# Transposed squares in 3 KB runs, and one interleaved sequence up to chunk 2

## The chip, the cores and the metric

The kernel runs on one core of one Trainium2 chip. The metric is device microseconds of that core for one launch. The inputs lie in the chip's memory and the output goes back there.

## The reference

```python
# attention: x (4, 4096, 192), weight_gen (4, 4096, 8 heads, 7 taps), all float32
w = softmax(weight_gen, axis=-1)
x_pad = six rows of zeros ahead of each batch of x
out[b, s, h, :] = sum over k of w[b, s, h, k] * x_pad[b, s + k, h, :]    # 24 columns a head
# feed-forward on the 16384 rows: w_in (192, 2048), w_out (2048, 192)
h = out @ w_in
g = maximum(0.01 * h, h)
result = g @ w_out
```

It is a causal convolution of seven taps whose weights differ by row and head, and then two matrix products with a leaky ReLU between them. Both products are made at more than the precision of one pass: every operand is cut into an upper half (the type fp32r) and the rest, and the products of the halves are summed.

## The kernel before

**Chunks, pairs, steps.** The 16384 rows are 32 chunks of 512. Chunk c has the convolution (`conv_ops`), the split into halves (`split_h`, `split_l`), the transposition (`squares` and `spread_squares`, which leave it in the tile `xx`), and eight *pairs* i of 256 of the 2048 hidden columns. Step n = 8c + i is `step(n)`: `mm1` makes the hidden columns of pair i into two PSUM tiles `hp` (18 matmuls), `act` turns each into `gh` (ACT) and `gl` (DVE), and `mm2` multiplies an earlier pair's `gh` and `gl` into `po` (20 matmuls). In a step with i = 0 two pairs go through `mm2` together (40 matmuls) and finish the chunk before, which `evacuate` then copies to `ot` in pieces of four copies on ACT per step. TensorE (PE) does nothing else but these matmuls.

**Transposition.** For every chunk but the first, DVE transposes 32 x 32 squares inside 32 partitions (two instructions, one for each half, `split` to `sq`), and then 16 DMAs carry the squares from `sq` to the partitions of `xx` where they belong. `xx` has two buffers, `sq` and `split` one. The first chunk goes through TensorE instead (`first_transposes`).

**Preparing the weights.** In the first 75 us the engines also turn the two weight matrices, which come as float64 words, into halves: 16 pieces (eight of w_in, called IN below, eight of w_out, called OUT), each in five stages: r (two reads on ACT), w (three DVE instructions at L119, L121 and L125), o (rounding up, at L133), u (upper half, L152 or L154) and l (lower half, L158). A stage has a DVE form (O, U, L) beside the usual one on GpSimd (POOL) or ACT. `mm1` of pair i waits for IN i, `mm2` for OUT i.

**What sets the order.** Instructions are queued on each engine in the order in which the Python code calls them. The string START is that order up to some step: each letter is one action (a stage of the next weight piece, one convolution operation of chunk 0 (d, e, g) or 1 (p), the first transposition T, the split c and v, the transposes t and m and the DMAs x of chunk 1), and `s` is the next step. START holds ten steps, 0 to 9; from there `step` itself calls everything, with these lines for a chunk c + 1:

```python
m = i - {1: 5, 2: 4, 3: 2}.get(c, 1)
if i == 0: feed(c + 1, 2 * K)              # the rest of the convolution of chunk c + 1, on POOL
if m == 0: split_h(c + 1); split_l(c + 1, nc.gpsimd)
if m == 1: squares(c + 1, 0); squares(c + 1, 1); spread_squares(...)
if m >= 0: feed(c + 2, 3)
```

So chunk 2 is split in step 13 (i = 5 of chunk 1) and transposed and sent in step 14, chunk 3 in steps 20 and 21. The softmax weights come in eight pieces of two chunks; piece 1 (chunks 2 and 3) is worked on in steps 0, 1, 6 and 7.

**Waits that the order makes.** `ps_h` has four PSUM banks, given in turn to every tile that asks: the two `hp` of a step and the tile `t` of every w. A tile waits until the one four before it is done with, so w's that stand between two steps decide which `gl` or which w the next step waits for. DMAs of the SP queue are issued one after the other.

Of the kernel before, what the change touches and what calls it, by code (L numbers as in the profile page):

```python
# [9 lines left out]
F32 = mybir.dt.float32  # L10
# [7 lines left out]
P = 128  # L18
# [6 lines left out]

C0 = 1

START = "ASdeegdegddegddeeeeddegpggrgwgdgeOgdrepggeeduprgldpdwopTwurwpsLorwrpopurOulupplwsLwOprsOurlwpwuorsouurlwlOrwlurwlswprooucLouwtUvmosrLwrUlswoUOlxUlsLss"


@with_exitstack
def conv_attention_moe_kernel(
# [140 lines left out]
    def load_weights(q):  # L173
        r0 = piece[q] * R
        wt[q] = win.tile([P, R, HK], F32, tag="wt", name="wt")
        nc.sync.dma_start(out=wt[q], in_=w_rows[:, r0:r0 + R, :])
# [26 lines left out]
    def softmax_max(q):  # L203
        mx[q] = win.tile([P, R * H, 1], F32, tag="mx", name="mx")
        sm[q] = win.tile([P, R * H, 1], F32, tag="sm", name="sm")
        nc.vector.tensor_reduce(out=mx[q], in_=grouped(q, ALL), axis=AX.X, op=ALU.max)  # L206

    def softmax_sub(q, eng):
        eng.tensor_tensor(  # L209
            out=grouped(q, ALL), in0=grouped(q, ALL), in1=spread(mx[q], ALL), op=ALU.subtract  # L210
        )
# [53 lines left out]
    xx = {}  # L265

    def new_xx(c):
        xx[c] = xtp.tile([P, 2, NB, TOK], F32R, tag="xx", name="xx", bufs=2)

    def first_transposes():  # L270
        new_xx(0)
        for b in range(NB):
            t = ps_h.tile([P, TOK], F32, tag="h", name="ta")
            for j in range(J):
                nc.tensor.transpose(  # L275
                    out=t[:, j * P:(j + 1) * P],
                    in_=twice[:, j, b].rearrange("p u d -> p (u d)"), identity=ident,
                )
            h, l = xx[0][:, 0, b, :], xx[0][:, 1, b, :]
            nc.scalar.copy(out=h, in_=t)  # L280
            nc.vector.tensor_tensor(out=l, in0=t, in1=h.bitcast(F32), op=ALU.subtract)

# [2 lines left out]
    def split_h(c):  # L285
        split[c] = xtp.tile([P, 2, J, D], F32R, tag="split", name="split")
        nc.scalar.copy(out=split[c][:, 0], in_=att[c])  # L287

    def split_l(c, eng):
        h, l = split[c][:, 0], split[c][:, 1]  # L290
        eng.tensor_tensor(out=l, in0=att.pop(c), in1=h.bitcast(F32), op=ALU.subtract)  # L291

    def squares(c, i):

        if i == 0:
            sq[c] = xtp.tile([P, 2, D // BK, J, BK], F32, tag="sq", name="sq")
        nc.vector.transpose(  # L297
            out=sq[c][:, i],
            in_=split[c][:, i].bitcast(F32).rearrange("p j (b d) -> p b j d", d=BK),
        )  # L300

    def spread_squares(c, engs):

        new_xx(c)
        dst = xx[c].bitcast(F32).rearrange("p i b t -> p (i b) t")
        n = 0
        for k in range(NK):
            src = sq[c][k * BK:(k + 1) * BK].rearrange("p i (b v) j t -> p v (i b) (j t)", v=2)
            for g in range(NK):
                engs[n % len(engs)].dma_start(  # L310
                    out=dst[g * BK:(g + 1) * BK, :, k * P:(k + 1) * P], in_=src[:, g % 2]
                )
                n += 1

# [2 lines left out]
    def mm1(q):  # L317

        c, i = divmod(q, NQ)
        h, l = xx[c][:, 0], xx[c][:, 1]  # L320
        passes = []
        for b in range(NB):
            passes += [(wi_h[:, b, i, :], h[:, b, :]), (wi_h[:, b, i, :], l[:, b, :])]
            passes.append((wi_l[:, b, i, :], h[:, b, :]))
        for u in range(2):
            hp[2 * q + u] = ps_h.tile([P, TOK], F32, tag="h", name="hp")
        for m, (w, r) in enumerate(passes):
            for u, s in enumerate(HALVES):
                nc.tensor.matmul(  # L329
                    out=hp[2 * q + u], lhsT=w[s], rhs=r[s],  # L330
                    start=(m == 0), stop=(m == len(passes) - 1),
                )
# [90 lines left out]
    with tc.manual_schedule():  # L423
        warm = const.tile([P, 1], F32, name="warm")
        nc.vector.memset(warm, 0.0)
        nc.scalar.activation(out=warm, in_=warm, func=AF.Exp)
        load_weights(0)
        load_words(order[0], nc.scalar)
        load_rows(0)
        for key in order[1:4]:  # L430
            load_words(key)
        make_identity(nc, ident)
        sm_q = {}
        for q in range(1, NPIECE):
            sm_q[max(0, 2 * q - 3)] = q
        NP = NCH * NQ

        convs = []

        def feed(c, n):  # L440

            while n > 0:
                if not convs or convs[-1][1] is None:
                    last = convs[-1][0] if convs else 1
                    if last + 1 > min(c, NCH - 1):
                        return
                    convs.append([last + 1, conv_ops(last + 1, nc.gpsimd, "tmp")])
                ops = convs[-1][1]
                if next(ops, ops) is ops:
                    convs[-1][1] = None  # L450
                else:
                    n -= 1

        outs = {}

        def step(q):

            c, i = divmod(q, NQ)
            if i == 0 and c in sm_q:
                load_weights(sm_q[c])  # L460
                load_rows(sm_q[c])
            if i == 1 and c in sm_q:
                softmax_max(sm_q[c])
                softmax_sub(sm_q[c], nc.gpsimd)
            mm1(q)
            for u in range(2):
                act(2 * q + u)
            if i == 0 and q > 0:
                mm2([2 * q - 4, 2 * q - 3])
                mm2([2 * q - 2, 2 * q - 1])  # L470
                outs[c - 1] = evacuate(c - 1)
                run(outs[c - 1], 1)
            elif i >= 2:
                mm2([2 * q - 4, 2 * q - 3])
            if i > 0 and c - 1 in outs:
                run(outs[c - 1], 4)
            if c > 0:

                m = i - {1: 5, 2: 4, 3: 2}.get(c, 1)
                if i == 0:  # L480
                    feed(c + 1, 2 * K)
                if c + 1 < NCH:
                    if m == 0:
                        split_h(c + 1)
                        split_l(c + 1, nc.gpsimd)
                    if m == 1:
                        squares(c + 1, 0)
                        squares(c + 1, 1)
                        spread_squares(c + 1, [nc.sync, nc.scalar] if c == 1 else [nc.sync])
                if m >= 0:  # L490
                    feed(c + 2, 3)
            if i == 6 and c in sm_q:
                softmax_exp(sm_q[c])
            if i == 7 and c in sm_q:
                softmax_sum(sm_q[c])
                softmax_div(sm_q[c], nc.gpsimd)

        w0 = ps_o.tile([P, J * H, K], F32, tag="m0", name="w0")
        conv0 = dict(
            d=conv_ops(0, nc.vector, "h", 0, 2, ps_h, w0),  # L500
            e=conv_ops(0, nc.vector, "h", 2, J - C0, ps_h, w0),
            g=conv_ops(0, nc.gpsimd, "tmp0", J - C0, J),
            p=conv_ops(1, nc.gpsimd, "tmp"),
        )
        n = 0
        for what in START:
            if what in stages:
                prepare(what)
            elif what == "A":
                softmax_max(0)  # L510
                softmax_sub(0, nc.vector)
                softmax_exp(0)
            elif what == "S":
                softmax_sum(0)
                softmax_div(0, nc.vector, slice(0, J - C0), w0[:, 0:(J - C0) * H, :])
                softmax_div(0, nc.gpsimd, slice(J - C0, R))
            elif what in conv0:
                run(conv0[what], 1)
            elif what == "T":
                first_transposes()  # L520
            elif what == "c":
                split_h(1)
            elif what == "v":
                split_l(1, nc.gpsimd)
            elif what in "tm":
                squares(1, "tm".index(what))
            elif what == "x":
                spread_squares(1, [nc.sync])
            elif what == "s":
                step(n)  # L530
                n += 1
        for n in range(n, NP):
            step(n)
        mm2([2 * NP - 4, 2 * NP - 3])
        mm2([2 * NP - 2, 2 * NP - 1])
        run(evacuate(NCH - 1))
# [33 lines left out]
```

## Time and profile before

| what | us |
|---|---|
| median of three runs | 1217.04 (1215.18 to 1217.26) |
| the profiled execution's own time | 1211.91 |
| its span, first to last instruction | 1210.1 |
| PE busy | 1154.7 (95%) |
| ACT, POOL, DVE busy | 883.1, 802.3, 607.1 |
| PE waits for the DMAs `xx<-sq` | 15.9 in 5 waits |

The busy share of PE is an average over stages. The profile is best read by stretches: the start, until the first step of chunk 1; then the stretches up to the first steps of chunks 2, 3 and so on; and the tail behind the last matmul.

### The profile page before, as it was taken

Reading aid. Unit: us, or ns where it says so; the run is one execution under the profiler, and the core shown is the slowest. Engines: PE = TensorE matmul, PEld = TensorE weight load, DVE = VectorE, ACT = ScalarE, POOL = GpSimd, SP = SyncE. Lnnn points to the kernel's source line nnn. Section 1 sums busy time; section 2 is a strip of 40 time slices with the busy share of each in tenths; the row PEclk is TensorE's granted clock in tenths of the full one; section 3 lists DMA queues with packets and bytes.
Section 4 is the critical chain, followed back from the end, with each engine's and each line's share of the span. In section 5 each row is a group of like instructions: output and inputs, shape, how many; then the busy total and the mean of one; then the engine's idle time right before and its main releaser. Section 6 shows DMA issues by size and latency. Waiting matters only on the chain.

```text
span 1210.1 us, 24837 instructions
## 1 busy us (share of the span) xinstructions
PE 1154.7 (95%) x9740; PEld 958.6 (79%) x9740; DVE 607.1 (50%) x905; ACT 883.1 (73%) x1936; POOL 802.3 (66%) x524
## 2 busy tenths in 40 slices
PE   2887989999999999999999999999999999999997
PEld 1676868888888888888888888888888888888885
DVE  8973435445454444545444454444445444544443
ACT  3855647887777778777777777778877777877775
POOL 7868378766666876666687666678766668866300
PEclk9899989999999999999999999999999999999999
DMA  4543042422324242232423323242331324222210
GB/s 146 156 119 66 1 119 66 118 58 52 98 48 120 66 108 65 54 93 54 119 66 92 81 49 93 58 120 66 77 93 44 96 64 119 66 66 43 48 43 27
DMA packets 118307, 94.94 MB, mean 78 GB/s; under 512 B 9391, under 2 KB 111791, under 8 KB 116398
## 3 DMA queue, kind: packets, MB, share of 16 engines
q1 hardware_dynamic: 116110, 92.18, 30.1%
q10 hardware_dynamic: 2080, 1.18, 0.5%
q8 instruction: 76, 1.25, 0.4%
q14 instruction: 41, 0.34, 0.1%
HBM read 31.98 MB, written 12.58 MB: 37 GB/s over the span
## 4 chain that ended last, share of the span: by engine, by line
PE 91%; DVE 3%; SPq 2%; DMA 1%; ACT 1%; issue 1%; POOL 0%; ACTq 0%; DVEq 0%
PE po L357 47%; PE hp L329 43%; SPq L310 2%; DMA xx<-sq 1%; ACT hp L336 1%; DVE sq L297 0%; DVE h L246 0%; DVE gl L340 0%; ACT gh L338 0%; DVE acc L256 0%; DVE t L121 0%; DVE bits L125 0%; DVE t L119 0%; PE ta L275 0%; DMA wt<-in_weight_gen_dram 0%
## 5 line engine op out<-in xcount | busy, mean ns | idle before, releaser
L357 PE MATMUL po<-gh,wo 64*128 64x512 f32 x3072 | 633.4, 393 | 0.0
L340 DVE TENSOR_TENSOR gl<-hp,gh 128x512 fp32r<-128x512 f32 x512 | 353.0, 690 | 542.0 <-ACT gh L338 540.8
L329 PE MATMUL hp<-xx,wi_h 64*128 64x512 f32 x3072 | 581.5, 396 | 25.7 <-DMA xx<-sq 15.9
L357 PE MATMUL po<-gl,wo 64*128 64x512 f32 x2048 | 554.4, 392 | 0.0
L357 PEld LDWEIGHTS po<-gh,wo 64*128 64x128 f32 x3072 | 479.3, 185 | 59.7
L329 PEld LDWEIGHTS hp<-xx,wi_h 64*128 64x128 f32 x3072 | 435.0, 186 | 91.4 <-issue 15.4
L329 PE MATMUL hp<-xx,wi_l 64*128 64x512 f32 x1536 | 476.2, 396 | 0.0
L336 ACT ACTIVATE hp<-hp 128x512 f32<-128x512 f32 x512 | 300.2, 586 | 203.2 <-PE hp L329 203.2
L357 PEld LDWEIGHTS po<-gl,wo 64*128 64x128 f32 x2048 | 377.9, 185 | 39.7
L256 POOL TENSOR_TENSOR acc<-acc,tmp 128x768 f32<-128x768 f32 (+1 forms) x191 | 347.2, 1818 | 14.3
L338 ACT CAST gh<-hp 128x512 fp32r<-128x512 f32 x512 | 300.5, 587 | 16.2
L329 PEld LDWEIGHTS hp<-xx,wi_l 64*128 64x128 f32 x1536 | 285.3, 186 | 30.5 <-DVE wi_l L158 0.4
L246 POOL TENSOR_TENSOR tmp<-xt,wt 128x768 f32<-128x768 f32 (+1 forms) x192 | 290.7, 1514 | 12.2
L395 ACT COPY ot<-z 32x128 f32<-32x128 f32 x752 | 223.4, 297 | 11.6 <-DVE z L379 0.9
L291 POOL TENSOR_TENSOR split<-acc,split 128x768 fp32r<-128x768 f32 x31 | 57.4, 1850 | 185.3 <-ACT split L287 185.3
L370 ACT COPY sa<-po 128x512 f32<-128x512 f32 x64 | 37.6, 587 | 59.9 <-PE po L357 59.9
L209 POOL TENSOR_TENSOR wt<-wt,mx 128x448 f32<-128x448 f32 x15 | 14.7, 977 | 99.2 <-DVE mx L206 96.6
L371 DVE TENSOR_TENSOR sa<-po,sa 128x512 f32<-128x512 f32 x64 | 43.0, 672 | 46.3 <-ACT sa L370 46.3
L297 DVE STREAM_TRANSPOSE sq<-split 128x768 f32<-128x768 f32 x62 | 56.8, 953 | 0.0
L246 POOL TENSOR_TENSOR acc<-xt,wt 128x768 f32<-128x768 f32 (+1 forms) x32 | 48.5, 1515 | 0.2
L395 POOL COPY ot<-z 32x128 f32<-32x128 f32 x8 | 2.7, 332 | 62.0 <-DVE z L379 61.8
L222 POOL TENSOR_TENSOR wt<-wt,sm 128x448 f32<-128x448 f32 (+1 forms) x16 | 15.3, 959 | 19.4 <-DVE sm L219 19.4
(50 smaller groups left out, 266.1 us busy)
## 6 DMA issues: line engine op xcount, KB each, us to landing
xx<-sq SPq DMA_DIRECT2D x488, 96.0 KB, 2.3
xt<-in_x_dram SPq DMA_DIRECT2D x14, 1344.0 KB, 6.5
out_dram<-ot SPq DMA_DIRECT2D x32, 384.0 KB, 2.5
wt<-in_weight_gen_dram SPq DMA_DIRECT2D x16, 224.0 KB, 3.2
wo_raw<-in_moe_w_out_dram SPq DMA_DIRECT2D x8, 384.0 KB, 3.5
wi_raw<-in_moe_w_in_dram SPq DMA_DIRECT2D x14, 192.0 KB, 3.4
xt<-in_x_dram SPq DMA_DIRECT2D x1, 960.0 KB, 5.0
xx<-sq ACTq DMA_DIRECT2D x8, 96.0 KB, 3.8
```

Source lines behind the costliest of these rows:

```text
L246: eng.tensor_tensor(out=ov, in0=xv, in1=wk, op=ALU.mult)
L256: eng.tensor_tensor(out=acc, in0=acc, in1=out, op=ALU.add)
L291: eng.tensor_tensor(out=l, in0=att.pop(c), in1=h.bitcast(F32), op=ALU.subtract)
L297: nc.vector.transpose(out=sq[c][:, i], in_=split[c][:, i].bitcast(F32).rearrange("p j (b d) -> p b j d", d=BK),)
L329: nc.tensor.matmul(out=hp[2 * q + u], lhsT=w[s], rhs=r[s], start=(m == 0), stop=(m == len(passes) - 1),)
L336: nc.scalar.activation(out=t, in_=t, func=AF.Prelu, alpha=0.01)
L338: nc.scalar.copy(out=g_h[n], in_=t)
L340: nc.vector.tensor_tensor(out=g_l[n], in0=t, in1=g_h[n].bitcast(F32), op=ALU.subtract)
L357: nc.tensor.matmul(out=po[which, u], lhsT=wo[s, f, w], rhs=g[n][s], start=(f == 0 and m == 0), stop=(f == NF - 1 and m == len(passes) - 1),)
L370: nc.scalar.copy(out=a, in_=po[which, 0])
L371: nc.vector.tensor_tensor(out=a, in0=po[which, 1], in1=a, op=ALU.add)
L395: engs[n % len(engs)](out=ot[k * BK:(k + 1) * BK, :, a * BK:(a + 1) * BK], in_=src[:, k])
```

## The change

It has three parts. First, `sq` and `xx` are laid out anew. Each of the 16 DMAs of a chunk carried 32 partitions of six runs of 512 bytes; now it carries 32 partitions of one run of 3 KB. `xx` has the block of 128 rows outermost, so `mm1` reads its right operand as four runs of 128 elements, and DVE makes the squares in four instructions of 384 elements in place of two of 768. Second, START grows from 10 steps to 16: it now holds the loading and the softmax of piece 1 (K, k, M, E, D), the convolutions of chunks 2 and 3 (q, 26 operations) and the split, the squares and the DMAs of chunk 2 (C, V, y, Y, X). The weight stages are ordered anew too: three U and one L fewer on DVE. Third, from chunk 3 on the split stands in pair 1 and the squares in pair 2 for every chunk. The DMAs of chunk 2 all go to SP; before, half of them went to the queue of ACT.

```diff
-START = "ASdeegdegddegddeeeeddegpggrgwgdgeOgdrepggeeduprgldpdwopTwurwpsLorwrpopurOulupplwsLwOprsOurlwpwuorsouurlwlOrwlurwlswprooucLouwtUvmosrLwrUlswoUOlxUlsLss"
+START = "ASgdeddeedddggedregpwpdgdrwegggekeodgggeedoegrgedupedlprruwTrowlpulwsKwroupOswlpuLopsrUlOwrppsuOrwlupowrrOulwwlrOuplpoMscuwutlrwvosumrEowlorLulwuODquqqqqLqqxssqLqqqqqssssCyVqqqqsqqqqqqqYqqXsss"
...
-        xx[c] = xtp.tile([P, 2, NB, TOK], F32R, tag="xx", name="xx", bufs=2)
+        xx[c] = xtp.tile([P, NK, 2, NB, P], F32R, tag="xx", name="xx", bufs=2)
...
-            sq[c] = xtp.tile([P, 2, D // BK, J, BK], F32, tag="sq", name="sq")
-        nc.vector.transpose(
-            out=sq[c][:, i],
-            in_=split[c][:, i].bitcast(F32).rearrange("p j (b d) -> p b j d", d=BK),
-        )
+            sq[c] = xtp.tile([P, 2, 2, NB, J, BK], F32, tag="sq", name="sq")
+        src = split[c][:, i].bitcast(F32).rearrange("p j (b v d) -> p v b j d", v=2, d=BK)
+        for v in range(2):
+            nc.vector.transpose(out=sq[c][:, v, i], in_=src[:, v])
...
-        dst = xx[c].bitcast(F32).rearrange("p i b t -> p (i b) t")
+        dst = xx[c].bitcast(F32).rearrange("p k i b t -> p k (i b t)")
+        src = sq[c].rearrange("p v i b j t -> p v (i b j t)")
         n = 0
         for k in range(NK):
-            src = sq[c][k * BK:(k + 1) * BK].rearrange("p i (b v) j t -> p v (i b) (j t)", v=2)
             for g in range(NK):
                 engs[n % len(engs)].dma_start(
-                    out=dst[g * BK:(g + 1) * BK, :, k * P:(k + 1) * P], in_=src[:, g % 2]
+                    out=dst[g * BK:(g + 1) * BK, k], in_=src[k * BK:(k + 1) * BK, g % 2]
                 )
...
-            passes += [(wi_h[:, b, i, :], h[:, b, :]), (wi_h[:, b, i, :], l[:, b, :])]
-            passes.append((wi_l[:, b, i, :], h[:, b, :]))
+            h, l = xx[c][:, :, 0, b, :], xx[c][:, :, 1, b, :]
+            passes += [(wi_h[:, b, i, :], h), (wi_h[:, b, i, :], l), (wi_l[:, b, i, :], h)]
...
-            if c > 0:
-
-                m = i - {1: 5, 2: 4, 3: 2}.get(c, 1)
+            if c > 1:
                 if i == 0:
                     feed(c + 1, 2 * K)
                 if c + 1 < NCH:
-                    if m == 0:
+                    if i == 1:
                         split_h(c + 1)
                         split_l(c + 1, nc.gpsimd)
-                    if m == 1:
+                    if i == 2:
                         squares(c + 1, 0)
                         squares(c + 1, 1)
-                        spread_squares(c + 1, [nc.sync, nc.scalar] if c == 1 else [nc.sync])
-                if m >= 0:
+                        spread_squares(c + 1, [nc.sync])
+                if i > 0:
                     feed(c + 2, 3)
...
+            elif what == "q":
+                feed(3, 1)
```

On the SP queue the order of the DMAs behind the weight loads changes as follows; the first group of `xx<-sq` is that of chunk 1, the second that of chunk 2 (`wt` and `xt` are the loads of a softmax piece and its rows, `out_dram` is a result).

```order
-L310 DMA xx<-sq 32x6x128 x16
+L311 DMA xx<-sq 32x768 x16
 L176 DMA wt<-in_weight_gen_dram 128x448
 L184 DMA xt<-in_x_dram 128x2688
-L310 DMA xx<-sq 32x6x128 x8
+L311 DMA xx<-sq 32x768 x16
 L401 DMA out_dram<-ot 128x768
```

Chunk 2's eight DMAs of the ACT queue have moved to SP, ahead of the same result, and every shape is now one run a partition.

On ACT, the instructions around the split of chunk 2 in the kernel before begin with the four copies that end step 13 and go on to the DMAs at the end of step 14 (`hp` and `gh` are `act`, `ot` are copies of `evacuate`).

```order
L395 COPY ot<-z 32x4x32 x4
L287 CAST split<-acc 128x768
L336 ACTIVATE hp<-hp 128x512
L338 CAST gh<-hp 128x512
L336 ACTIVATE hp<-hp 128x512
L338 CAST gh<-hp 128x512
L395 COPY ot<-z 32x4x32 x4
L310 DMA xx<-sq 32x6x128 x8
```

In the changed kernel the same split stands between the copies that end step 11 and the `act` of step 12.

```order
L395 COPY ot<-z 32x4x32 x4
L288 CAST split<-acc 128x768
L336 ACTIVATE hp<-hp 128x512
L338 CAST gh<-hp 128x512
L336 ACTIVATE hp<-hp 128x512
L338 CAST gh<-hp 128x512
L395 COPY ot<-z 32x4x32 x4
```

It has moved two steps ahead, and no DMA is issued on ACT behind it.

On DVE, this is what stands in the kernel before from the `gl` of step 3 (first row) to the `gl` of step 4 (last row): three w's and one rounding.

```order
L340 TENSOR_TENSOR gl<-hp,gh 128x512 x2
L119 TENSOR_SCALAR t<-mag 128x384
L121 TENSOR_SCALAR t<-t 128x384
L125 SCALAR_TENSOR_TENSOR bits<-wo_raw,t 128x384
L133 ISA bits<-bits,rnd 128x768
L119 TENSOR_SCALAR t<-mag 128x384
L121 TENSOR_SCALAR t<-t 128x384
L125 SCALAR_TENSOR_TENSOR bits<-wi_raw,t 128x384
L119 TENSOR_SCALAR t<-mag 128x384
L121 TENSOR_SCALAR t<-t 128x384
L125 SCALAR_TENSOR_TENSOR bits<-wo_raw,t 128x384
L340 TENSOR_TENSOR gl<-hp,gh 128x512 x2
```

In the changed kernel a rounding and two w's follow the `gl` of step 3, and then the rows below, up to the `gl` of step 4 (`mx` is the maximum of softmax piece 1).

```order
L133 ISA bits<-bits,rnd 128x768
L119 TENSOR_SCALAR t<-mag 128x384
L121 TENSOR_SCALAR t<-t 128x384
L125 SCALAR_TENSOR_TENSOR bits<-wi_raw,t 128x384
L119 TENSOR_SCALAR t<-mag 128x384
L121 TENSOR_SCALAR t<-t 128x384
L125 SCALAR_TENSOR_TENSOR bits<-wo_raw,t 128x384
L133 ISA bits<-bits,rnd 128x768
L206 TENSOR_REDUCE mx<-wt 128x64
L340 TENSOR_TENSOR gl<-hp,gh 128x512 x2
```

Between the two steps DVE now has four w's, three roundings and a maximum in place of three w's and one rounding; elsewhere ahead of step 8 it has less.

## Rows read from the trace of the kernel before

**Rows 1.** Busy time by stretch: PE, PEld, DVE, ACT, POOL, granted clock, DMA share, GB/s

```profile
24.35:74.37 50.02, 40.80 (x265) 29.32 (x265) 44.13 (x77) 36.07 (x72) 39.62 (x37) 0.86 0.57 156
74.37:125.81 51.44, 41.08 (x325) 38.34 (x327) 21.82 (x33) 27.61 (x61) 43.93 (x28) 0.90 0.28 73
125.81:169.91 44.10, 38.54 (x308) 32.37 (x306) 16.17 (x23) 26.65 (x60) 25.63 (x16) 0.93 0.28 73
169.91:1200.26 1030.35, 1030.35 (x8832) 855.57 (x8830) 500.18 (x717) 782.12 (x1723) 673.16 (x411) 1.00 0.30 74
```

**Rows 2.** The chain that ended last: start, us; each chunk's double `mm2`

```profile
78.05 4.67 PE po L357 x40
...
125.81 4.90 PE po L357 x40
...
169.91 5.03 PE po L357 x40
...
205.75 4.67 PE po L357 x40
...
241.21 4.67 PE po L357 x40
```

**Rows 3.** Timeline of PE, steps 16 and 24: start, us, [idle before, releaser]

```profile
119.11 0.76 PE L329 MATMUL hp<-xx,wi_h 64*128 64x512 f32 x1 [7.70 <-DMA xx<-sq]
...
164.41 0.76 PE L329 MATMUL hp<-xx,wi_h 64*128 64x512 f32 x1 [5.00 <-DMA xx<-sq]
```

**Rows 4.** Timeline of ACT and DVE: step 11's copies, chunk 2's split and squares

```profile
93.77 1.21 ACT L395 COPY ot<-z 32x128 f32<-32x128 f32 x4
...
103.64 0.84 ACT L287 CAST split<-acc 128x768 fp32r<-128x768 f32 x1
...
107.44 1.83 DVE L297 STREAM_TRANSPOSE sq<-split 128x768 f32<-128x768 f32 x2
```

**Rows 5.** Timeline of the SP queue, chunk 3's transfers

```profile
152.90 11.02 SPq L310 DMA_DIRECT2D xx<-sq  x16
```

**Rows 6.** DMA issues by line: duration ns min/median/max; landing of L310's

```profile
L310 SPq DMA_DIRECT2D xx<-sq x488: 585/610/2247, 62.7 to 1153.5; - x163
DMA to landing us min/median/max: 2.2/2.3/4.4
...
L401 SPq DMA_DIRECT2D out_dram<-ot x32: 332/349/712, 116.8 to 1206.7; - x32
...
L95 SPq DMA_DIRECT2D wi_raw<-in_moe_w_in_dram x14: 595/604/748, 2.1 to 48.1; - x14
...
L98 SPq DMA_DIRECT2D wo_raw<-in_moe_w_out_dram x8: 368/379/599, 16.6 to 60.5; - x8
```

**Rows 7.** Stretches as in rows 1: chunk 3's transfers; a load of a softmax piece

```profile
153.00:164.00 11.00, 6.41 (x55) 5.15 (x51) 2.76 (x4) 5.15 (x12) 10.52 (x7) 0.99 0.63 127
...
165.00:175.00 10.00, 9.43 (x61) 7.83 (x62) 1.91 (x3) 3.07 (x6) 7.17 (x5) 0.72 0.56 203
```

**Rows 8.** Timeline of DVE between steps 0 and 1

```profile
32.81 1.09 DVE L133 CUSTOM_DVE_ANT_0 bits<-bits,rnd 128x768 uint16<-128x768 uint16 x1
33.82 0.55 DVE L119 TENSOR_SCALAR t<-mag 128x384 f32<-128x384 f32 x1
...
35.53 0.61 DVE L206 TENSOR_REDUCE mx<-wt 128x64 f32<-128x448 f32 x1
36.06 1.37 DVE L340 TENSOR_TENSOR gl<-hp,gh 128x512 fp32r<-128x512 f32 x2
```

**Rows 9.** Timeline of PE: what steps 4 and 8 waited for

```profile
50.35 0.74 PE L329 MATMUL hp<-xx,wi_h 64*128 64x512 f32 x3 [1.22 <-DVE bits L125]
...
75.72 0.69 PE L329 MATMUL hp<-xx,wi_h 64*128 64x512 f32 x3 [0.90 <-DMA xx<-sq]
```

**Rows 10.** Timeline of POOL: first and last operation of chunk 2's convolution (13)

```profile
76.98 1.54 POOL L246 TENSOR_TENSOR acc<-xt,wt 128x768 f32<-128x768 f32 x1
...
98.17 1.86 POOL L256 TENSOR_TENSOR acc<-acc,tmp 128x768 f32<-128x768 f32 x1
```

More of the change, by code (lines that the diff above doesn't have):

```diff
@@ L278, in first_transposes @@
                 )
-            h, l = xx[0][:, 0, b, :], xx[0][:, 1, b, :]
+            t = t.rearrange("p (j t) -> p j t", j=J)
+            h, l = xx[0][:, :, 0, b, :], xx[0][:, :, 1, b, :]
             nc.scalar.copy(out=h, in_=t)
@@ L319, in mm1 @@
         c, i = divmod(q, NQ)
-        h, l = xx[c][:, 0], xx[c][:, 1]
         passes = []
         for b in range(NB):
-            passes += [(wi_h[:, b, i, :], h[:, b, :]), (wi_h[:, b, i, :], l[:, b, :])]
-            passes.append((wi_l[:, b, i, :], h[:, b, :]))
+            h, l = xx[c][:, :, 0, b, :], xx[c][:, :, 1, b, :]
+            passes += [(wi_h[:, b, i, :], h), (wi_h[:, b, i, :], l), (wi_l[:, b, i, :], h)]
         for u in range(2):
@@ L433, in conv_attention_moe_kernel @@
         sm_q = {}
-        for q in range(1, NPIECE):
-            sm_q[max(0, 2 * q - 3)] = q
+        for q in range(2, NPIECE):
+            sm_q[2 * q - 3] = q
         NP = NCH * NQ
@@ L520, in conv_attention_moe_kernel @@
                 first_transposes()
[L521 to L524, printed above, removed]
+            elif what == "K":
+                load_weights(1)
+            elif what == "k":
+                load_rows(1)
+            elif what == "M":
+                softmax_max(1)
+                softmax_sub(1, nc.gpsimd)
+            elif what == "E":
+                softmax_exp(1)
+            elif what == "D":
+                softmax_sum(1)
+                softmax_div(1, nc.gpsimd)
+            elif what == "q":
+                feed(3, 1)
+            elif what in "cC":
+                split_h(1 + "cC".index(what))
+            elif what in "vV":
+                split_l(1 + "vV".index(what), nc.gpsimd)
             elif what in "tm":
                 squares(1, "tm".index(what))
-            elif what == "x":
-                spread_squares(1, [nc.sync])
+            elif what in "yY":
+                squares(2, "yY".index(what))
+            elif what in "xX":
+                spread_squares(1 + "xX".index(what), [nc.sync])
             elif what == "s":
```

## The prediction

> **What bounds the kernel now.** The busy shares name TensorE, and the first question is whether it waits at all. So I read the busy time by stretch first. From the double `mm2` of step 24 to the last matmul PE is busy for every one of 1030.35 us, 8832 matmuls at 116.7 ns, at full clock [rows 1]. Nothing that leaves the matmuls as they are can gain there. What can be gained lies in the three stretches ahead of it: 50.0, 51.4 and 44.1 us, at a mean granted clock of 0.86, 0.90 and 0.93, so that some of their matmuls ran at 1.2 GHz in place of 2.4.
>
> Second, the chain that ended last. A steady chunk is the distance of two double `mm2` in it, 241.21 − 205.75 = 35.46 us. From step 8 to step 16 it took 125.81 − 78.05 = 47.76, from step 16 to step 24 44.10, and the one after that 35.84 [rows 2]. The three together lose 127.70 − 3 x 35.46 = **21.3 us**: 12.3, 8.6 and 0.4.
>
> Third, PE's own timeline, for what ended the waits: both times a DMA `xx<-sq`, after 7.70 us idle at step 16 and 5.00 at step 24 [rows 3]. That is less than the 12.3 and 8.6 lost, because a second, shorter wait follows and the matmuls behind it come at 1.2 GHz. I take from this that a stall of several us costs about 2 us more than its length.
>
> Fourth, what was late. Chunk 2's split on ACT was issued at 103.64 and its two transposes on DVE ended at 107.44 + 1.83 = 109.3 [rows 4]; only then could 16 DMAs go out, and PE ran dry at 119.11 − 7.70 = 111.4. Chunk 3's 16 DMAs took SP 11.0 us from 152.90, while PE ran dry at 164.41 − 5.00 = 159.4 [rows 3, 5]. POOL had finished chunk 2's convolution at 98.17 + 1.86 = 100.0 [rows 10]; the split stood behind the copies of step 13. So order and issue time make these stalls, not work that is missing.
>
> **The change part by part.**
>
> *Issue of a chunk's DMAs.* An `xx<-sq` of 32 x 6 runs takes SP 0.610 us, 16 of them 11.0 with the gaps, and each lands 2.3 later [rows 5, 6]. The new form, one 3 KB run a partition, is not in the trace. The nearest row by shape is `out_dram<-ot`, one 3 KB run on each of 128 partitions, 0.349. With a gap of 0.05 that makes 16 x 0.40 = 6.4 us. The upper bound is the old 11.0. Which is nearer? `wi_raw`, with three runs on each of 64 partitions, takes 0.604, and `wo_raw`, with two on each of 128, 0.379 [rows 6]: the number of runs alone does not set the time, but both rows with one or two runs a partition are near 0.36. I take 6.4. Bandwidth won't bind: in the old bursts the DMA engines were 63% busy at 127 GB/s, that is 200 GB/s at full share, and at the load of long rows 203/0.56 = 360 [rows 7]. The 1.5 MB of a chunk need some 5 us at a rate between the two, less than the issue.
>
> *Chunk 3's split three steps earlier.* It moves from step 20 to step 17, its squares from step 21 to 18. A step takes 38 x 116.7 ns = 4.43 us, so the transfers start 13.3 us earlier, and the last data came at 152.90 + 11.0 + 2.3 = 166.2 against 159.4 needed. Margin 6.5 us even at the old issue time. POOL must have chunk 3's convolution by then. It starts behind chunk 2's split at about 99.7 (below) and takes 23.05 us like chunk 2's (76.98 to 100.03, [rows 10]): 122.8. The split's place in step 17 is about 122. The stall goes: **8.6 us**.
>
> *The start, to step 8.* PE waits here for DVE, whose queue holds the w's (33.82 to 35.53, 1.71 us each), the roundings (about 1.0) and the `gl` (1.37 a step) [rows 8]. Ahead of step 0 DVE has one w more and one rounding less, so step 0 is 0.4 us later. Between the `gl` of steps 0 and 1 the old order had an l, two w's, a rounding and a maximum; now a w and a rounding. Step 2 waited for that `gl`, up to 36.76 [rows 8]; now the `gl` comes when ACT delivers, 1.5 to 2 us earlier. Step 4 gives it back: four w's stand ahead of it, its two banks are freed by the first two, and these follow the `gl` of step 3. With that `gl` over at 45.9 and a rounding and two w's behind it, step 4 starts at 45.9 + 1.0 + 3.4 = 50.3, and it started at 50.35 [rows 9]. Then a rounding, two w's, a rounding and the maximum (6.0) put the `gl` of step 4 at 57.7, about 1 us later than before, and step 5 waits for it. By step 6 the two orders are level again. Step 8 waited for chunk 1's DMAs until 75.72 [rows 9]. Now the last transposes end at about 64.2, and 64.2 + 6.4 + 2.3 = 72.9; its banks come free at 73.3. That is 2.4 us earlier. I count **1.5**, since the granted clock of 0.86 in this stretch shows low stretches whose number the new pauses may change; bounds −4 and +5.
>
> *Chunk 2.* The softmax sums of piece 1 stand on DVE behind the w's of step 6, at about 70.7, and the division on POOL ends at 71.7. Then 23.05 us of convolution: 94.8. The split's slot on ACT, behind step 11's copies, is 93.77 + 1.21 − 2.4 = 92.6 [rows 4], so ACT waits 2 us for POOL. Queued behind the split are the `act` of step 12 (four operations, 2.3 us), the `gl` and the second half of the squares: 94.8 + 0.8 + 2.3 + 0.7 + 1.1 = 99.7 (two transposes of 384 elements taken at half of 1.83 and a little). PE does not feel the late `act`, since step 14 needs its result and banks only at about 101. DMAs: 99.7 + 6.4 + 2.3 = 108.4. PE runs dry at 111.4 − 2.4 = 109.0. The stall goes, with 0.6 us to spare: **12.3 us**, and with it the 0.4 behind.
>
> *At no cost.* Two more transposes a chunk add some 0.4 us on DVE, which is idle half of the steady stretch (500 of 1030 us busy, [rows 1]); they would count only in a chunk where DVE is late. Four runs in place of one in `mm1`'s right operand are in no row; I take nothing, and price it below.
>
> **Sum.** 21.3 + 1.5 = 22.8, less 0.8 for a margin as thin as 0.6: 22 us. The profiled execution took 1211.9 (span 1210.1 and 1.8 around it), so 1189.9. The median of the runs shown is 5.1 above that execution; I give the forecast for such a median: **1195 us**.
>
> **The rivals.**
>
> *The issue time stays at 11.0.* Chunk 1's data then come at 64.2 + 11.0 + 2.3 = 77.5 and step 8 starts 4 us later than above. Chunk 2's order still moves two steps, and its transfers, started behind step 12's `gl` at 101.5, land at 114.8 with PE dry at 113: 2 us, and 2 of low clock. Together 8 lost of 22: 1203. The Trainium skill speaks for it: "DMA: Bandwidth & Descriptors", section "Anatomy of one DMA — SWDGE (gpsimd) path", says that descriptor generation is a small cost and that many descriptors can be emitted before the increment shows. By that rule fewer runs would not shorten the issue. The rows agree in part: `wo_raw` has 256 runs and 0.379, but `wi_raw` has 192 and 0.604 [rows 6]. 0.15.
>
> *POOL or DVE is late at chunk 2.* Chunk 2's chain has 0.6 us of slack, and each us by which the softmax sums or the convolution slip beyond it is a us of stall. For it speaks that POOL and DVE are both near full in the start (39.6 and 44.1 of 50 us, [rows 1]), and that I placed every instruction there by hand. 4 us late cost 4 + 2: 1201. 0.13.
>
> *The start gains more*, because low stretches drop out: 5 in place of 1.5, some 1190 or a little less. 0.08.
>
> *The strided operand slows `mm1`* (the other side). 4608 of 9728 matmuls read `xx`. If four runs cost each of them d, the kernel loses 4608 d; at d = 22/4608 us = 4.8 ns, 4% of 116.7, the whole gain is gone, and at 10 ns the time is 1195 + 46 = 1241. Against it: PE's pace is the same for `mm1` and `mm2`, 116.7 ns, longer than 512 columns of two concurrent matmuls need at 2.4 GHz (106.7 each), so reading has some room. No row has such an operand, so I leave it 0.05, of which 0.03 beyond 4.8 ns.
>
> **Chances and range.** Likeliest, 0.59: both stalls gone, the start within a few us, 1190 to 1200 by itself. 0.2% of 1217 (2.4 us) is about what a measurement can tell from no change. Of the strided case 0.01 stays faster, 0.01 is no change and 0.03 slower, so faster is 0.59 + 0.15 + 0.13 + 0.08 + 0.01 = 0.96, same 0.01, slower 0.03. For 8 in 10 the range takes in the better start and most of both late cases: 1187 to 1204.
>
> **What would show it.** Right: issues of `xx<-sq` near 0.35 us and bursts near 6.5; no PE wait for `xx<-sq` longer than 1 us at steps 16 and 24; distances of the double `mm2` near 35.5 from step 8 on; step 8's at about 75.7; PE still fully busy at 116.7 ns behind it. Wrong: bursts of 11 us (first rival), ACT's split of chunk 2 waiting for POOL well beyond 95 (second), or a chunk distance above 35.5 in the steady part (fourth). Should PE's granted clock be low in more of the first 75 us, the start is what I missed.

## The result and the profile after

The changed kernel takes **1196.09 us** (median of 4 runs, 1194.02 to 1197.19), beside 1216.11 for the kernel before on the same chip (4 runs, 1213.70 to 1217.26). The ratio is 0.9836, 95% interval 0.9814 to 0.9858: 20.0 us, 1.6% faster. The forecast was 1195. The profiled execution took 1194.02 (span 1192.2), 17.9 us less than the profiled execution before.

The profile, its first lines and PE's share:

```profile
span 1192.2 us, 24936 instructions
...
PE 1148.1 (96%) x9740; PEld 1101.9 (92%) x9740; DVE 608.3 (51%) x963; ACT 883.7 (74%) x1939; POOL 803.2 (67%) x525
```

Busy time by stretch, cut at the end of step 8's last wait and at the double `mm2` of steps 16 and 24 (PE, PEld, DVE, ACT, POOL, granted clock, DMA share, GB/s), which answers to [rows 1] (in those rows the first cut stands at step 8's first matmul, ahead of its last wait):

```profile
25.25:76.96 51.71, 39.20 (x267) 28.69 (x267) 44.66 (x77) 34.86 (x69) 44.73 (x40) 0.93 0.44 115
76.96:116.49 39.53, 39.53 (x324) 33.16 (x326) 18.94 (x30) 27.42 (x61) 35.42 (x23) 0.96 0.30 90
116.49:151.96 35.47, 35.47 (x307) 34.52 (x306) 16.67 (x26) 26.68 (x60) 31.51 (x19) 1.00 0.33 92
151.96:1182.50 1030.54, 1030.54 (x8837) 1002.94 (x8835) 502.78 (x773) 782.58 (x1724) 670.55 (x410) 1.00 0.27 74
```

From that wait on PE is never idle. The second and third stretch were 51.4 (0.9 of it that last wait) and 44.1 us long and are now 39.5 and 35.5, fully busy. Behind them nothing changed: 1030.54 us for 8837 matmuls, 116.6 ns each; PEld's busy time there rose from 856 to 1003 us. That need not be the change's doing: from 300 to 1100 us the two traces of the changed kernel itself have 779 and 734, with PE fully busy in both. What sets it no run here tells. The start is not shorter.

The chain that ended last shows the same by the double `mm2` of each chunk, as in [rows 2]:

```profile
79.97 5.53 PE po L357 x40
...
116.49 4.67 PE po L357 x40
...
151.96 4.67 PE po L357 x40
...
187.42 4.67 PE po L357 x40
```

The distances are 36.52, 35.47 and 35.46, together 107.45 where they were 127.70: **20.25 us gained**. Step 8's own comes at 79.97, **1.92 later** than before. Behind step 32 another 0.4 is lost. 20.25 − 1.92 − 0.4 = 17.9, the difference of the two profiled executions.

What did not come as forecast is in three views. First, the issues of a chunk's transfers, with their landing, then bursts 1 to 3 on SP's queue (start, us), which answer to [rows 5, 6]:

```profile
L311 SPq DMA_DIRECT2D xx<-sq x496: 507/590/2103, 63.7 to 1134.4; - x166
...
DMA to landing us min/median/max: 2.0/2.2/4.5
```

```profile
63.66 11.47 SPq L311 DMA_DIRECT2D xx<-sq  x16
...
102.08 10.40 SPq L311 DMA_DIRECT2D xx<-sq  x16
...
131.78 10.06 SPq L311 DMA_DIRECT2D xx<-sq  x16
```

An issue takes 0.590 us, not 0.35; it was 0.610. A burst takes 10.1 to 11.5, not 6.5. The time to landing counts from the start of the issue: chunk 2's burst of issues ends at 112.5, its last issue began at 111.9, and this transfer landed at 114.0. Second, PE at step 8, the last place where it waits (compare [rows 9]):

```profile
75.65 0.46 PE L329 MATMUL hp<-xx,wi_h 64*128 64x512 f32 x1 [2.35 <-DVE wo L158]
...
76.96 0.70 PE L329 MATMUL hp<-xx,wi_h 64*128 64x512 f32 x3 [0.84 <-DMA xx<-sq]
```

Both waits are for chunk 1's data, though the first is put down to DVE. The first matmul reads 64 partitions, the last of which come with the 14th transfer, and the second reads the other 64, up to the 16th. These landed at 75.4 and 76.7, and PE went on at 75.65 and 76.96. In the second trace of the changed kernel the first of the two waits bears the name:

```profile
78.41 0.47 PE L329 MATMUL hp<-xx,wi_h 64*128 64x512 f32 x1 [1.45 <-DMA xx<-sq]
```

Third, chunk 2's way from POOL over ACT and DVE (compare [rows 4, 10]):

```profile
93.19 1.85 POOL L256 TENSOR_TENSOR acc<-acc,tmp 128x768 f32<-128x768 f32 x1
...
96.52 1.22 ACT L395 COPY ot<-z 32x128 f32<-32x128 f32 x4
97.76 0.84 ACT L288 CAST split<-acc 128x768 fp32r<-128x768 f32 x1
...
101.44 1.03 DVE L301 STREAM_TRANSPOSE sq<-split 128x384 f32<-128x384 f32 x2
```

POOL is done with the convolution at 95.04, and ACT's split comes 2.7 us behind it, right after the copies of step 11 that stand ahead of it. So ACT came last here, not POOL.

### The profile page after: what moved, and what is told of

Same layout as the page of the kernel before. It is cut to its first block, busy times and chain, and to the rows that moved or that the text cites. A ratio compares the mean times of both kernels' runs of the same rounds, so it can differ in the third digit from the quotient of the medians.

```text
span 1192.2 us, 24936 instructions
## 1 busy us (share of the span) xinstructions
PE 1148.1 (96%) x9740; PEld 1101.9 (92%) x9740; DVE 608.3 (51%) x963; ACT 883.7 (74%) x1939; POOL 803.2 (67%) x525
## 4 chain that ended last, share of the span: by engine, by line
PE 94%; DVE 2%; DMA 1%; ACT 1%; SPq 1%; issue 0%; DVEq 0%; ACTq 0%
PE po L357 49%; PE hp L329 45%; SPq L311 1%; DMA wi_raw<-in_moe_w_in_dram 1%; DVE gl L340 0%; ACT hp L336 0%; ACT gh L338 0%; DVE t L121 0%; DVE acc L256 0%; DMA wt<-in_weight_gen_dram 0%; DVE t L119 0%; DVE h L246 0%; DVE bits L125 0%; DMA xx<-sq 0%; DVE ot L395 0%
## 5 line engine op out<-in xcount | busy, mean ns | idle before, releaser
L357 PE MATMUL po<-gh,wo 64*128 64x512 f32 x3072 | 624.8, 392 | 0.0
L329 PE MATMUL hp<-xx,wi_h 64*128 64x512 f32 x3072 | 571.0, 395 | 13.4 <-DVE bits L125 5.7
L357 PE MATMUL po<-gl,wo 64*128 64x512 f32 x2048 | 538.2, 392 | 0.0
L357 PEld LDWEIGHTS po<-gh,wo 64*128 64x128 f32 x3072 | 493.1, 184 | 12.4
L329 PEld LDWEIGHTS hp<-xx,wi_h 64*128 64x128 f32 x3072 | 456.7, 185 | 31.7 <-DVE gl L340 5.6
L329 PE MATMUL hp<-xx,wi_l 64*128 64x512 f32 x1536 | 451.3, 394 | 0.0
L301 DVE STREAM_TRANSPOSE sq<-split 128x384 f32<-128x384 f32 x124 | 60.6, 544 | 1.4 <-ACT split L288 1.4
```

The costliest lines, as they stand in the source:

```text
L301: nc.vector.transpose(out=sq[c][:, v, i], in_=src[:, v])
L329: nc.tensor.matmul(out=hp[2 * q + u], lhsT=w[s], rhs=r[s], start=(m == 0), stop=(m == len(passes) - 1),)
L357: nc.tensor.matmul(out=po[which, u], lhsT=wo[s, f, w], rhs=g[n][s], start=(f == 0 and m == 0), stop=(f == NF - 1 and m == len(passes) - 1),)
```

## The experiments

The theory was that nearly all of the gain is the order (chunks 2 and 3 handed out two and three steps earlier) and that the layout brings next to nothing, because SP's issue paces a burst and hardly got shorter. The rival: the long runs relieve the DMA engines, and the layout carries a part of its own.

**The layout alone.** The kernel before with the new `sq`, `xx`, transposes, transfers and right operand of `mm1`; its sequence and step code kept. The lines show two of the places:

```diff
-        xx[c] = xtp.tile([P, 2, NB, TOK], F32R, tag="xx", name="xx", bufs=2)
+        xx[c] = xtp.tile([P, NK, 2, NB, P], F32R, tag="xx", name="xx", bufs=2)
...
-                    out=dst[g * BK:(g + 1) * BK, :, k * P:(k + 1) * P], in_=src[:, g % 2]
+                    out=dst[g * BK:(g + 1) * BK, k], in_=src[k * BK:(k + 1) * BK, g % 2]
```

> The kernel before, with the new layout of the transposed squares alone (16 transfers of 3 KB runs, two transposes per half of a split, the strided operand of mm1); its order of work is kept. Theory (the gain is the order of chunks 2 and 3; the layout is worth next to nothing, since an issue of such a transfer costs SP 0.59 us with runs of 3 KB, where it cost 0.61 with runs of 512 bytes): 16 x 0.02 = 0.3 us less ahead of chunk 3's data, nothing else; the time is that of the kernel before less 0 to 1 us, a ratio of 0.999 to 1.000, and the two waits for xx at steps 16 and 24 stay near 7.7 and 5.0 us. Rival (longer runs relieve the DMA engines, so a burst lands earlier): the burst of chunk 2 over two queues and that of chunk 3 shorten, the two waits fall by some 2 to 3 us each, and the ratio is 0.995 to 0.997.

1209.81 us beside 1212.74, ratio 0.9968 (0.9955 to 0.9981): **2.9 us** by the medians, 3.9 (2.3 to 5.5) by the ratio. That is the rival's range, and the theory's 0 to 1 us is outside the interval. The trace says where, by the chain and by PE at step 16:

```profile
81.22 4.79 PE po L357 x40
...
126.24 4.66 PE po L357 x40
...
169.41 5.04 PE po L357 x40
```

```profile
121.00 0.76 PE L329 MATMUL hp<-xx,wi_h 64*128 64x512 f32 x1 [6.30 <-DMA xx<-sq]
```

Chunk 2's eight issues on ACT, in the kernel before and here:

```profile
L310 ACTq DMA_DIRECT2D xx<-sq x8: 688/904/1164, 109.3 to 116.0; - x8
```

```profile
L311 ACTq DMA_DIRECT2D xx<-sq x8: 514/609/888, 112.7 to 118.3; - x8
```

Chunk 2 took 45.02 in place of 47.76, chunk 3 43.17 in place of 44.10: 2.7 and 0.9. The rival's 2 to 3 us a stall came at chunk 2 alone. In the old order chunk 2's transfers go out on two queues at once, and there the short runs did hold: ACT's issues had a median of 0.90 us in the kernel before and have 0.61 here, and SP's eight, beside them, went from 7.04 us to 6.22. So the theory falls in this part: where two queues issue, the layout relieves them.

**The order alone.** The changed kernel with the old layout; the edit is the reverse of the one above. It ran twice, the second time beside the changed kernel on one chip: the first time it lay 2 us over the changed kernel by the medians and 4 by the ratios, each of which is to other runs of the kernel before.

> The changed kernel with the old layout of the transposed squares (runs of 512 bytes); the new order is kept. Theory (order alone): a burst of 16 issues takes 0.3 to 0.6 us longer, which delays step 8 by as much and leaves steps 16 and 24 with a wait below 1 us; 0.5 to 2 us over the changed kernel, ratio to the kernel before 0.984 to 0.986. Rival (the layout carries a part): chunk 1's burst, which goes out beside the loads of words, lands 2 us or more later and chunk 2's data arrive after step 16 is due; 3 to 6 us over the changed kernel, ratio 0.986 to 0.989.

1197.96 us, ratio 0.9869 (0.9848 to 0.9890), the rival's range.

> The changed kernel itself, unaltered, as the mark for the three kernels beside it. Both theories: a ratio of 0.982 to 0.986 to the kernel before. The start (up to step 8) is expected to differ from the first trace by up to 3 us, since the granted clock fell at other places between 30 and 45 us in the traces of the kernels with the same start, and step 16 to follow step 8 by 36 to 37 us.

> The changed kernel with the old layout (runs of 512 bytes) once more, beside the changed kernel. In the first look it lay 4 us over the changed kernel by the two ratios, while its trace showed only 1.2 us that the layout explains (0.6 us in the burst ahead of step 8, 0.6 us at step 16). Theory A (bursts on one queue, paced by the issue): 0.5 to 2 us over the changed kernel. Theory B (the layout is worth as much here as in the old order, where it gave 3.9 us): 3 to 5 us over it.

The changed kernel: 1195.71 us (1194.80 to 1196.80), ratio 0.9837 (0.9815 to 0.9860). With the old layout: 1197.81 (1197.61 to 1198.86), ratio 0.9856 (0.9834 to 0.9878). **2.1 us**, just above theory A's range and below theory B's; no run of the one lies among the runs of the other. One wait of it can be seen, at step 16, which the changed kernel does not have:

```profile
118.29 0.69 PE L329 MATMUL hp<-xx,wi_h 64*128 64x512 f32 x3 [0.83 <-DMA xx<-sq]
```

The first run of this kernel has the same wait of 0.83. So the order alone gives some 18 of the 20 us, and the layout 2 on top of it.

**Chunk 3's hand-out put back.** In the step code:

```diff
-                    if i == 1:
+                    if i == {2: 4, 3: 2}.get(c, 1):
...
-                    if i == 2:
+                    if i == {2: 5, 3: 3}.get(c, 2):
```

> The changed kernel, but chunk 3's split is handed out at pair 4 and its squares at pair 5, and chunk 4's at pairs 2 and 3, as in the kernel before; all else as changed. Theory (the wait at step 24 was the time of handing out): chunk 3's issues begin three pairs later, near 145 us, its last data land near 157.5, and step 24, due at 149.6, waits some 8 us, with about 2 us more behind it at a lower clock: 8 to 10 us over the changed kernel, ratio 0.990 to 0.992. Rival (the layout or the rest of the order made room for chunk 3 too): less than 4 us over the changed kernel.

1204.44 us, ratio 0.9917 (0.9887 to 0.9948), as the theory has it. Step 24 waits again, though not the 8 us expected:

```profile
157.20 0.76 PE L329 MATMUL hp<-xx,wi_h 64*128 64x512 f32 x1 [4.26 <-DMA xx<-sq]
```

By the chain, step 16 to step 24 is 42.81 against 35.47: 7.3 us. The idle time is 4.3 and a second wait 0.5; the rest is the low clock behind it (granted 0.51 between 157 and 162). Chunk 4, which the edit puts back too, loses nothing: 35.47 to step 32.

**Chunk 2's hand-out two steps later.** In the written sequence:

```diff
-START = "ASgdeddeedddggedregpwpdgdrwegggekeodgggeedoegrgedupedlprruwTrowlpulwsKwroupOswlpuLopsrUlOwrppsuOrwlupowrrOulwwlrOuplpoMscuwutlrwvosumrEowlorLulwuODquqqqqLqqxssqLqqqqqssssCyVqqqqsqqqqqqqYqqXsss"
+START = "ASgdeddeedddggedregpwpdgdrwegggekeodgggeedoegrgedupedlprruwTrowlpulwsKwroupOswlpuLopsrUlOwrppsuOrwlupowrrOulwwlrOuplpoMscuwutlrwvosumrEowlorLulwuODquqqqqLqqxssqLqqqqqssssssCyVqqqqsqqqqqqqYqqXs"
```

> The changed kernel, but in the sequence that is written out the split, the squares and the transfers of chunk 2 stand two steps later. Theory (chunk 2's data now land just as step 16 is due, with no slack): its issues begin near 110.9 instead of 102.1 us, the last data land near 123.6, step 16, due at 114.2, waits some 9 us, with about 2 us more behind it at a lower clock: 9 to 11 us over the changed kernel, ratio 0.991 to 0.993. Rival (there is slack that the trace doesn't show, or the wait falls into time that PE loses anyway): less than 5 us over the changed kernel.

1204.84 us, ratio 0.9930 (0.9907 to 0.9952), the upper end of the theory's range. Step 16:

```profile
120.78 0.76 PE L329 MATMUL hp<-xx,wi_h 64*128 64x512 f32 x1 [7.60 <-DMA xx<-sq]
```

Step 8 to step 16 is 46.29 against 36.52: 9.8 us. So each hand-out, put back by itself, brings back most of its stall: 7.3 and 9.8 us, where the change had taken away 8.6 and 11.2.

**What an issue costs by form.** A kernel that only issues transfers, 16 of a form, each burst behind the landing of the one before:

```python
for form, engs in forms:
    for n in range(16):
        d, s = form(n)
        engs[n % len(engs)].dma_start(out=d, in_=s)
    nc.vector.memset(dst, 0.0)
```

> A kernel that computes nothing of the reference: it only issues transfers, 16 of one form in a burst, each burst behind the landing of the one before it, so that the duration of an issue on the queue can be read for each form by itself. Bursts in order, all on SP where not said: (1) 32 partitions x 3 KB from SBUF to SBUF (the changed kernel's form); (2) 32 x 6 runs of 512 bytes (the form before); (3) 32 x one run of 512 bytes; (4) 32 x 6 KB; (5) 16 x 3 KB; (6) 64 x 3 KB; (7) 128 x 3 KB; (8) 32 x 3 KB from DRAM; (9) 128 x 3 KB from DRAM; (10) 32 x 3 KB to DRAM; (11) 128 x 3 KB to DRAM; (12) form 1 on ACT's queue; (13) form 1 on SP and ACT in turn; (14) form 2 on SP and ACT in turn; (15) form 1 on SP again. Theory A (an issue costs a fixed time per transfer unless the DMA engines hold it up): near 0.6 us for forms 1 to 5, 12 and 15 whatever the runs and bytes, and longer for forms 6, 7 and 9 only because 16 engines need 1.2 us or more for their bytes. Theory B (it costs by the number of partitions or descriptors that are written): forms 3 and 4 as form 1, form 5 about half, form 6 about double. Theory C (by bytes): form 3 near 0.1 us, form 4 near 1.2 us. Of forms 10 and 11 the prediction's 0.35 us is expected only if the direction to DRAM sets it. Forms 13 and 14: with short runs the two queues hold each other up (0.8 to 0.9 us an issue, as in the kernel before at chunk 2), with long runs less (0.6 to 0.77, as in the layout alone).

The issue rows of forms 1 to 11 without 5, in this order, then ACT's half of forms 13 and 14 (duration ns min/median/max, first and last start us):

```profile
L116 SPq DMA_DIRECT2D dst<-src x16: 565/592/605, 15.3 to 24.8; - x16
...
L116 SPq DMA_DIRECT2D dst<-src x16: 585/606/668, 40.0 to 49.9; - x16
...
L116 SPq DMA_DIRECT2D dst<-src x16: 560/588/591, 65.1 to 74.6; - x16
...
L116 SPq DMA_DIRECT2D dst<-src x16: 507/912/990, 89.4 to 102.2; - x16
...
L116 SPq DMA_DIRECT2D dst<-src x16: 461/596/781, 144.0 to 153.7; - x16
...
L116 SPq DMA_DIRECT2D dst<-src x16: 482/942/951, 172.2 to 185.7; - x16
...
L116 SPq DMA_DIRECT2D dst<-in_x_dram x16: 404/419/422, 202.7 to 209.6; - x16
...
L116 SPq DMA_DIRECT2D dst<-in_x_dram x16: 327/362/908, 224.9 to 236.0; - x16
...
L116 SPq DMA_DIRECT2D out_dram<-dst x16: 349/420/429, 256.8 to 263.8; - x16
...
L116 SPq DMA_DIRECT2D out_dram<-dst x16: 351/942/953, 278.6 to 291.9; - x16
...
L116 ACTq DMA_DIRECT2D dst<-src x8: 526/603/886, 334.2 to 339.4; - x8
...
L116 ACTq DMA_DIRECT2D dst<-src x8: 655/841/1041, 356.2 to 362.2; - x8
```

From SBUF to SBUF the median is 0.587 (form 5) to 0.596 from 16 partitions to 64, with one run of 512 bytes or of 3 KB; six runs cost 0.014 more. So between two ends in SBUF an issue costs a fixed time per transfer, as theory A has it. It missed form 4: 6 KB a partition took 0.91, and 128 partitions 0.94, and in both the shortest is 0.48 to 0.51 and the DMA engines were 76 and 79% busy over the stretch, so the issue is held up there. With one end in DRAM and 32 partitions it is 0.42, to and from. To DRAM the shortest of a burst is 0.349 with 32 partitions and 0.351 with 128. It is the first of the burst both times, with none just ahead of it on the queue, and this is where the prediction's 0.35 belongs. In the changed kernel, too, the result's DMA takes longer right behind the burst of chunk 2 than by itself:

```profile
112.57 0.53 SPq L401 DMA_DIRECT2D out_dram<-ot  x1
...
146.51 0.35 SPq L401 DMA_DIRECT2D out_dram<-ot  x1
```

The number of partitions makes no such difference until the DMA engines fall behind. From DRAM with 128 partitions the median of 0.36 lies between 0.33 for issues behind a pause and more for those behind one another. Two queues hold each other up with short runs (0.84 on either) and less with long ones (0.60, single issues up to 0.89), as at chunk 2 of the kernel before and of the layout alone. This kernel ran once.

**Every fourth transfer on ACT's queue,** first of chunk 1's burst (there `if what == "x" else [nc.sync]` follows), then of both written bursts:

```diff
-                spread_squares(1 + "xX".index(what), [nc.sync])
+                spread_squares(1 + "xX".index(what), [nc.sync] * 3 + [nc.scalar])
```

> The changed kernel, but of the 16 transfers of chunk 1 every fourth is issued by ACT's queue. Theory (a burst is paced by SP's issue, and chunk 2's data have no slack): SP's burst shrinks from 10.4 to near 7.8 us, mm1 of step 8 begins some 2.5 us earlier, and step 16, whose data come as before, then waits these 2.5 us; the time stays within 1 us of the changed kernel. Rival (the DMA engines pace the burst): step 8 isn't earlier at all, and ACT's four issues cost it up to 2.5 us. Rival (chunk 2 has slack after all): 2 to 3 us faster.

> The changed kernel with every fourth transfer of chunk 1 and of chunk 2 issued by ACT's queue. Theory (issue on SP paces both bursts): step 8 some 2.5 us earlier, chunk 2's last data land near 110 instead of 114.7 us, ahead of step 16, which follows step 8 by 35.5 to 36.5 us; 2 to 3.5 us faster than the changed kernel, ratio 0.980 to 0.983 to the kernel before. Rival (ACT's issues, some 2.4 us each time in its order, hold up its casts): no faster than the changed kernel, with PE waits for gl or gh behind step 7 or at steps 13 to 15.

Chunk 1's alone: 1193.96 us (1192.46 to 1195.66), ratio 0.9826 (0.9804 to 0.9848). Both: 1193.18 us (1191.08 to 1194.63), ratio 0.9815 (0.9791 to 0.9839), against 1195.71 of the changed kernel on the same chip: 1.8 and 2.5 us by the medians, the first with overlapping runs, both with overlapping intervals of the ratio. From chunk 1's first issue to the double `mm2` of step 8 it is 15.6 and 15.0 us here, and 16.3 and 16.0 in the two traces of the changed kernel: 0.4 to 1.3 us of the 2.5 expected. What the medians show beyond that lies within the spread of the start (last section). SP's waits in the first kernel say why:

```profile
SPq L311 <- DMA xx<-sq: 2.1, 1, 2.1
```

ACT reaches its four issues only at 69.2, and SP, with nine of its twelve out by 69.9, waits 2.1 us for one of ACT's to land. That step 16 would then wait in place of step 8 was wrong: chunk 2's burst began earlier too, at 100.72 in place of 102.08, and PE does not wait there. With both bursts split, chunk 2's takes SP 7.67 us:

```profile
103.28 7.67 SPq L311 DMA_DIRECT2D xx<-sq  x12
```

That is 0.64 us an issue, the pace of 16 in 10.4: the issue sets a burst's length. From step 8 to step 16 this brings nothing that can be told: 35.99 us, and 36.52 and 35.96 in the two traces of the changed kernel. This version is the fastest of all by its median, and its runs lie below those of the changed kernel on the same chip.

## Why the prediction came out as it did

*Issue of a chunk's DMAs: wrong.* The term was 6.4 us, taken from `out_dram<-ot` as the nearest row by shape; it measures 10.4 (11.5 at chunk 1). The step that failed is that choice. The row is near in its runs, but it goes to DRAM, and most of its issues stand alone on the queue; an end in DRAM lowers an issue from 0.59 to 0.42, and standing alone from there to 0.35. The trace of before showed the second already: right behind a burst of `xx<-sq` the row's issue took 0.71 (at 116.8) and 0.54 (at 164.0). It had no other issue from SBUF to SBUF than the old form's 0.610, and that was the nearest row. Why `wi_raw`, from DRAM too, has 0.604 [rows 6], none of the forms tells. The rule of the Trainium skill named there ("DMA: Bandwidth & Descriptors", section "Anatomy of one DMA — SWDGE (gpsimd) path") points the right way, though that section is about DMAs of the gpsimd path and these go out on SP: the trace agrees that fewer runs hardly shorten the issue, 0.606 against 0.592.

*The start: right up to step 5, wrong at step 8.* Step 4 was forecast at 50.3 and came at 50.09; step 5 waited for the `gl` of step 4 until 57.02, forecast 57.7. Step 8 was to start at 73.3; its second wait ended at 76.96, 3.7 later. The burst began half a microsecond earlier than placed (63.7, and with the second half of the squares at 64.3), but took 11.5 us in place of 6.4. At the pace of the later bursts (10.1 to 10.4) 16 issues make 3.7 to 4.0 of these 5.1; the rest is the third issue, which took 1.94 us, and why no run tells. Part of it comes back, because the sum added the 2.3 to landing to the end of the burst, while they count from the start of its last issue. In place of +1.5 the start gave −1.9 in this trace.

*Chunk 3: right.* Its stall of 8.6 us is gone at the old issue time too, as the margin of 6.5 said: with the old layout step 24 does not wait either.

*Chunk 2: right in the outcome, not in the way.* The softmax sums ended at 70.6 and the convolution at 95.04, forecast 70.7 and 94.8. But the forecast had ACT wait 2 us for POOL, from 92.6 on; ACT's copies of step 11 ended only at 97.7, some 5 us late, as PE was from step 8 on. So the transfers began at 102.1 in place of 99.7, and the last landed at 114.0 in place of 108.4. PE was through with step 15 not at 109.0 but at 114.2, for the same reason: 4.3 us at step 8's double `mm2`, and 1.1 more by step 16, behind a granted clock of 0.82 from 80 to 85 us. Of the 12.3 us 11.2 came. The first rival, whose premise is true, has the mechanism nearly right: step 8 some 4 us later, transfers from 101.5 on, PE's need at 113. Its stall did not come, because the low clock put PE's need 1.1 us later still, to 114.2, and because the data landed at 114.0 and not at 114.8. So of its 8 us, which end at 1203, only the 4 of step 8 are seen, and 1.1 of low clock behind it. What is left is a slack near zero: with the old layout, whose burst is 0.4 us longer, step 16 waits 0.83.

*At no cost: right.* 116.6 ns per matmul with the strided operand, 116.7 without; no DVE wait from the extra transposes.

*The layout's share was not in the sum as such.* It was there only through the issue time. What it brings, 2.1 us in the new order and 3 to 4 in the old, comes by 0.02 us less an issue, by 0.1 less to land, and in the old order by the two queues holding each other up less. In the new order the first traces of the two kernels differ by 0.7 us from chunk 1's first issue to step 8 and 0.6 from there to step 16, the second traces by 1.3 and 1.6. The 2.1 lies between 1.3 and 2.9; how it divides two traces each can't tell, and I leave it open.

*The sum.* Against the profiled executions 22 us were forecast and 17.9 came: step 8 makes 3.4 of the 4.1 missing (+1.5 against −1.9), the low clock behind it 1.1 and the stretch behind step 32 0.4, less the 0.8 that were held back for a thin margin. The median came close all the same, 1196.1 against 1195, because the changed kernel's profiled execution lies 2.1 below its median, where 5.1 was added. So the nearness of the two figures is partly luck.

## What to carry to other kernels

Price a transfer's issue by a row that has the same two ends (SBUF or DRAM) and stands on the queue as yours will, in a burst or alone; here the length of the runs and the number of partitions hardly moved it as long as the DMA engines kept up. When PE waits for data at the head of a chunk, first see whether the order could hand them out earlier: here that was worth 18 us and the layout 2. And when an earlier stage gets slower, ask which of the later hand-outs move along with it before adding up stalls.

## What the runs showed of the hardware

The start of one and the same kernel differs between executions. The stretch from 30 to 40 us in the two traces of the changed kernel, the first and the second one:

```profile
30.00:40.00 10.00, 7.10 (x56) 5.26 (x56) 7.93 (x13) 7.83 (x16) 7.90 (x7) 1.00 0.39 109
```

```profile
30.00:40.00 10.00, 7.04 (x35) 5.08 (x36) 6.98 (x12) 5.91 (x12) 7.88 (x7) 0.63 0.41 120
```

PE is busy for the same 7 us, with 56 matmuls at a granted clock of 1.00 and 35 at 0.63, between pauses of 0.6 to 1.6 us. Step 8's double `mm2` comes at 79.97 and 83.30, and the spans are 1192.2 and 1195.0: in these two the start makes the whole difference, a little over the 3 us expected of it. From step 8 to 16 the second has 35.96, where 36 to 37 were expected. Terms of one or two us in such a start can't be judged from one trace.

An issue on SP waits for the DMA engines once these are behind: from SBUF to SBUF 128 partitions of 3 KB take 0.48 at first and then 0.94. And issuing from two engines saves only the issue, as the Trainium skill says ("DMA: Bandwidth & Descriptors", section "Issuing engines are not separate DMA queues"); it calls that time usually small beside the transfer, but in these bursts 16 issues were 10.4 us of the 11.9 to the last landing. Moving four of them to another queue in both bursts gained 2.5 us by the medians, of which the traces show 1.0 to 1.3 ahead of step 8.
